# Reordering the first loads of a linear-attention and token-MLP kernel: one DMA ring held back, two weight chunks moved forward, DMA transposes held behind a copy

## The chip, the cores and the metric

The kernel runs on one core of one Trainium2 chip. The metric is the device time of one execution in microseconds (us), median over several runs. Beside it stands the profile of one execution; its span is about 1.8 us shorter than the time of the same run, and all times inside it are counted from the start of its span. The engines are PE (matrix multiply), PEld (its weight loads), DVE (vector), ACT (scalar), POOL and SP (which here only issues DMAs). DMAs are issued on two rings, SP's and ACT's. With one core there is no die to compare with, so the runs call a run slow when it is over 1.5% above the fastest of the same kernel.

## The reference, cut to what matters

```python
def reference(A_x, A_wqkv, A_wo, B_x, B_w1, B_b1, B_w2, B_b2, gate_w):
    x = A_x                                     # 1 x 2048 x 512, bf16
    g = _sigmoid((x * gate_w).sum(-1, keepdims=True))
    # a: qkv = x @ wqkv; linear attention with 32 heads and phi(t) = (t+1 if t>0 else exp(t)) + 1e-6; then @ wo
    # b: layernorm(x), then an MLP over the token axis: 2048 -> 1792 (gelu) -> 2048
    return g * a + (1 - g) * b
```

Only the beginning concerns us. It computes k = x @ Wk for one tile of 128 tokens after another, and phi(k). For this PE needs x transposed, and Wk, whose 512 rows come in four chunks of 128 (wk0 to wk3).

## The kernel before

The first four x tiles (x0 to x3) are transposed by PE, the other twelve by DMA transposes. Six dummy matmuls keep PE busy until x0 is there.

```python
    load_x(nc.sync, 0, 1)
    load_x(nc.scalar, 1, 1)
    load_wk(nc.sync, 0)
    load_x(nc.scalar, 2, 1)
    load_x(nc.sync, 3, 1)
    for k, q in ((1, nc.scalar), (2, nc.sync), (3, nc.scalar)):
        load_wk(q, k)
    load_xT(4, 2)                       # DMA transposes, all on SP's ring
    load_xT(6, 2)
    load_x(nc.sync, 4, 4)
    # ... further loads on SP's ring, cut ...
    warm_up(6)                          # dummy 128x512 matmuls

    def transpose_tile(t, on_act):      # 4 PE transposes, one copy PSUM -> SBUF
        pt = bank("pt", BF16)
        for k in range(ND):
            nc.tensor.transpose(pt[:, k * P : (k + 1) * P], xs[:, t, k * P : (k + 1) * P], ident[:])
        # ... copy by ACT if on_act, else by DVE ...

    HEADS = 4
    transpose_tile(0, False)
    transpose_tile(1, True)
    transpose_tile(2, False)
    ln_step(0)
    for k in range(2):
        for t in range(HEADS - 1):
            k_part(t, (k,))             # one matmul: tile t with wk chunk k
    transpose_tile(HEADS - 1, True)
    ln_step(1)
    for t in range(HEADS):
        k_part(t, range(2 if t < HEADS - 1 else 0, ND))
        k_phi(t)
    # for t in range(HEADS, NT): k_part(t, ...), k_phi(t), g_tile(t - LAG), ...  cut
```

Of the kernel before, what the change touches and what calls it, by code (L numbers as in the profile page):

```python
# [10 lines left out]
BF16 = mybir.dt.bfloat16  # L11
# [4 lines left out]
def kernel(  # L16
# [13 lines left out]
    nc = tc.nc  # L30
    P = nc.NUM_PARTITIONS
# [6 lines left out]
    S, D = X.shape  # L38
    F = B_w1.shape[1]
    NT = S // P  # L40
    ND = D // P
# [4 lines left out]
    FB = 4  # L46
# [4 lines left out]
    w1_chunks = [(j, min(FB, NF - j)) for j in range(0, NF, FB)]  # L51
# [3 lines left out]
    wqkv_view = A_wqkv.rearrange("(k p) n -> p k n", p=P)  # L55
    wo_view = A_wo.rearrange("(j p) n -> p j n", p=P)
    w1_view = B_w1.rearrange("(t p) f -> p t f", p=P)
# [3 lines left out]
    wpool = ctx.enter_context(tc.tile_pool(name="wstream", bufs=4))  # L61
# [5 lines left out]
    def keep(shape, dtype, name):  # L67
        return persist.tile(shape, dtype, name=name, tag=name)

    def bank(name, dtype=FP32):  # L70
        return ps.tile([P, SC], dtype, name=name, tag="bank")

    xs = keep([P, NT, D], BF16, "xs")
    hs = keep([P, NT, D], BF16, "hs")
    xT = keep([P, ND, S], BF16, "xT")
    wq_sb = keep([P, ND, D], BF16, "wq_sb")
    wk_sb = keep([P, ND, D], BF16, "wk_sb")
    wv_sb = keep([P, ND, D], BF16, "wv_sb")
    wo_sb = keep([P, ND, D], BF16, "wo_sb")
# [32 lines left out]
    def mm(o, lhsT, rhs, start, stop, **kw):  # L112
        nc.tensor.matmul(o, lhsT=lhsT, rhs=rhs, start=start, stop=stop, **kw)  # L113
# [14 lines left out]
    def load_x(q, t0, n):  # L128
        q.dma_start(out=xs[:, t0 : t0 + n, :], in_=x_view[:, t0 : t0 + n, :])

    def load_wk(q, k):
        q.dma_start(out=wk_sb[:, k, :], in_=wqkv_view[:, k, D : 2 * D])

    def load_xT(t0, n):
        nc.sync.dma_start(
            out=xT[:, :, t0 * P : (t0 + n) * P], in_=X[t0 * P : (t0 + n) * P, :], transpose=True
        )

    load_x(nc.sync, 0, 1)
    load_x(nc.scalar, 1, 1)  # L140
    load_wk(nc.sync, 0)
    load_x(nc.scalar, 2, 1)
    load_x(nc.sync, 3, 1)
    for k, q in ((1, nc.scalar), (2, nc.sync), (3, nc.scalar)):
        load_wk(q, k)
    load_xT(4, 2)
    load_xT(6, 2)
    load_x(nc.sync, 4, 4)
    for t0, n in ((8, 4), (12, 4)):
        load_xT(t0, n)  # L150
        load_x(nc.sync, t0, n)
    nc.sync.dma_start(out=wq_sb[:], in_=wqkv_view[:, :, 0:D])
    w1c = []
    for c, (j0, nb) in enumerate(w1_chunks):
        w = wpool.tile([P, NT, FB * P], BF16, name="w1c", tag="wc")
        w1c.append(w)
        for t0 in range(0, NT, 8) if c == 0 else (0,):
            t1 = t0 + 8 if c == 0 else NT
            nc.sync.dma_start(
                out=w[:, t0:t1, : nb * P], in_=w1_view[:, t0:t1, j0 * P : (j0 + nb) * P]  # L160
            )
        if c == 0:
            nc.sync.dma_start(out=wv_sb[:], in_=wqkv_view[:, :, 2 * D : 3 * D])
            nc.sync.dma_start(out=wo_sb[:], in_=wo_view)

    nc.vector.memset(ones_f[:], 1.0)
    nc.vector.memset(mhalf[:], -0.5)
    nc.vector.memset(Z32[:], 0.0)
    nc.gpsimd.memset(ident[:], 0.0)
    nc.gpsimd.affine_select(  # L170
        out=ident[:], in_=ident[:], compare_op=ALU.not_equal, fill=1.0, base=0,
# [5 lines left out]
        out=maskQ[:], in_=maskH[:].rearrange("p (a m) -> p m a", m=2), op=ALU.max, axis=AX.X  # L177
# [12 lines left out]
    def warm_up(n, cols=SC):  # L190
        for _ in range(n):
            mm(wps[:, :cols], warm[:, 0:P], warm[:, :cols], True, True)

    act_warm = keep([P, 1], FP32, "act_warm")
    nc.scalar.activation(out=act_warm[:], in_=ones_f[:], func=ACT.Exp)
    warm_up(6)

    def transpose_tile(t, on_act):
        pt = bank("pt", BF16)
        for k in range(ND):  # L200
            nc.tensor.transpose(pt[:, k * P : (k + 1) * P], xs[:, t, k * P : (k + 1) * P], ident[:])  # L201
        dst = xT[:, :, t * P : (t + 1) * P]
        src = pt[:].rearrange("p (k s) -> p k s", k=ND)
        if on_act:
            nc.scalar.activation(out=dst, in_=src, func=ACT.Copy)
        else:
            nc.vector.tensor_copy(out=dst, in_=src)
# [13 lines left out]
    def k_part(t, ks):  # L221
        if t not in kaccs:
            kaccs[t] = bank("kacc")
        for k in ks:
            mm(
                kaccs[t][:], xT[:, k, t * P : (t + 1) * P], wk_sb[:, k, :],
                k == 0, k == ND - 1,
            )

    def k_phi(t):  # L230
        phi(pk[:, t, :], kaccs.pop(t))
# [46 lines left out]
    def ln_step(u):  # L278
        ln_stats(u)
        if u % TPC == TPC - 1:  # L280
            ln_rstd(u // TPC)

    HEADS = 4
    transpose_tile(0, False)
    transpose_tile(1, True)
    transpose_tile(2, False)
    ln_step(0)
    for k in range(2):
        for t in range(HEADS - 1):
            k_part(t, (k,))  # L290
    transpose_tile(HEADS - 1, True)
    ln_step(1)
    for t in range(HEADS):
        k_part(t, range(2 if t < HEADS - 1 else 0, ND))
        k_phi(t)
    LAG = 4
    LN_LAG = 3
# [156 lines left out]
    for j in range(NB0, NF):  # L454
        c, jj = divmod(j, FB)
# [18 lines left out]
        out=gg[:], in0=gth[:], scalar1=0.5, scalar2=0.5, op0=ALU.mult, op1=ALU.add  # L474
    )
    nc.vector.tensor_scalar(
        out=c1[:], in0=gth[:], scalar1=-0.5, scalar2=0.5, op0=ALU.mult, op1=ALU.add
# [3 lines left out]
    for t in range(NT):  # L481
        c, tl = divmod(t, TPC)
        aps = bank("aps")
        for j in range(ND):
# [3 lines left out]
            out=a_sc[:], in_=aps[:], func=ACT.Identity,  # L488
            scale=gg[:, t : t + 1], bias=c2[:, t : t + 1],
        )  # L490
        for c0, W in ((0, D - P), (D - P, P)) if t == NT - 1 else ((0, D),):
            cs = slice(c0, c0 + W)
            yps = bank("yps")
            for f in range(NF):
# [6 lines left out]
                out=ot[:, :W], in0=yps[:, :W], scalar=c1[:, t : t + 1], in1=a_sc[:, cs],  # L501
# [35 lines left out]
```

## Time and profile before

| | |
|---|---|
| time, median of 3 runs (later 4) | 164.49 us (164.51), 164.18 to 164.63 |
| span of the profile | 162.6 us |
| first x tile landed, first PE transpose | 3.69 us, 3.74 us |
| PE at full clock from | 5.73 us |
| last of the eight first loads landed | 6.83 us |
| tile 4's first k matmul | 9.05 us |
| last store landed, end of the span | 161.63 us, 162.59 us |

Landings are read from the semaphore records of the trace (a semaphore is a counter on which engines wait): a load has landed when the last of its 16 increments is there. The full clock begins where the trace's clock record goes from 0.5 to 1.0.

From the page of the kernel before: PE's share (part 1), what the DMA engines moved in 40 slices of 4.07 us (part 2), and the chain that ended last, by engine and by line (part 4).

```profile
...
PE 158.0 (97%) x823; PEld 72.9 (45%) x837; DVE 89.5 (55%) x210; ACT 63.3 (39%) x97; POOL 17.5 (11%) x34
...
GB/s 141 252 247 246 278 312 355 382 386 386 281 5 0 0 0 223 228 4 0 272 324 77 209 328 323 279 106 94 32 32 32 32 32 43 48 42 33 32 32 32
...
PE 96%; DMA 2%; issue 1%; DVE 0%
PE uacc L113 30%; PE yps L113 30%; PE kacc L113 9%; PE aps L113 8%; PE gacc L113 8%; PE qacc L113 8%; DMA xs<-in_A_x_dram 2%; PE pt L201 1%; PE denps L113 1%; PE kvps L113 0%; PE w2ps L113 0%; DVE ot L500 0%; PE pt L330 0%
```

PE is busy almost all of the span. The chain's share that is not PE lies in the first microseconds. Here is that chain in order of time, for the first 10 us of the kernel before; the columns are start, duration (both us), and what.

```profile
...
0.81 2.88 DMA xs<-in_A_x_dram
3.69 0.05 issue
3.74 1.46 PE pt L201 x12
5.20 1.63 PE kacc L113 x6
6.83 0.22 PE pt L201 x4
7.05 3.02 PE kacc L113 x14
```

By this reading the kernel waits 2.88 us for x0, and then PE works without a hole.

The timeline of PE in the kernel before, 2.4 to 7.2 us: start, duration, engine, line, operation, output and inputs, count, and in brackets the idle time before it and what ended that.

```profile
...
3.74 1.46 PE L201 MATMUL pt<-ident,xs 128*128 128x128 bf16 x12 [0.17 <-DMA xs<-in_A_x_dram]
4.99 1.84 PE L113 MATMUL kacc<-wk_sb,xT 128*128 128x512 bf16 x6
6.66 0.39 PE L201 MATMUL pt<-ident,xs 128*128 128x128 bf16 x4
6.89 0.60 PE L113 MATMUL kacc<-wk_sb,xT 128*128 128x512 bf16 x2
```

Twelve transposes, six k matmuls, four transposes, then the rest. Before 5.73 us the starts of two 128x512 matmuls lie 0.427 us apart, after it 0.216 us.

The last thing to read is the end, which nobody looked at before the result. There the engines meet at two barriers: with a drain (an instruction that does no work here) an engine joins a barrier, and then it waits until the barrier is released.

### The profile page before, as it was taken

How to read it: one execution, taken by the hardware profiler on the slowest of the kernel's cores; microseconds unless marked ns; L12 is line 12 of the kernel's file. 1: busy time of each engine (PE TensorE's matmuls, PEld its weight loads, DVE VectorE, ACT ScalarE, POOL GpSimd, SP SyncE). 2: the span in 40 equal slices, each digit the busy share in tenths (PEclk: the TensorE clock that was granted, in tenths of full speed). 3: DMA queues.
4: the chain of work that ended last, by engine and by line, in shares of the span. 5: the costliest groups of instructions: out<-in, count | busy, mean ns of one | idle time of the engine just before them, and what ended most of it. 6: DMA issues, size and time to landing. Idle time of an engine off the chain costs nothing.

```text
span 162.6 us, 2183 instructions
## 1 busy us (share of the span) xinstructions
PE 158.0 (97%) x823; PEld 72.9 (45%) x837; DVE 89.5 (55%) x210; ACT 63.3 (39%) x97; POOL 17.5 (11%) x34
## 2 busy tenths in 40 slices
PE   7999999999999999999999999999999999999992
PEld 2544444444444444444444444444444444444452
DVE  0599999967999999519995401166211111111112
ACT  3463386648667483212865113111122222111110
POOL 3000711200110000001415500050000000000000
PEclk9999999999999999999999999999999999999999
DMA  4999999999900006600892699732000001110001
GB/s 141 252 247 246 278 312 355 382 386 386 281 5 0 0 0 223 228 4 0 272 324 77 209 328 323 279 106 94 32 32 32 32 32 43 48 42 33 32 32 32
DMA packets 30057, 25.05 MB, mean 154 GB/s; under 512 B 7968, under 2 KB 29472, under 8 KB 30048
## 3 DMA queue, kind: packets, MB, share of 16 engines
q1 hardware_dynamic: 28032, 22.02, 42.9%
q0 software_dynamic: 1440, 2.38, 5.5%
q10 hardware_dynamic: 576, 0.52, 1.1%
q8 instruction: 6, 0.10, 0.2%
q14 instruction: 3, 0.02, 0.1%
HBM read 21.11 MB, written 2.23 MB: 144 GB/s over the span
## 4 chain that ended last, share of the span: by engine, by line
PE 96%; DMA 2%; issue 1%; DVE 0%
PE uacc L113 30%; PE yps L113 30%; PE kacc L113 9%; PE aps L113 8%; PE gacc L113 8%; PE qacc L113 8%; DMA xs<-in_A_x_dram 2%; PE pt L201 1%; PE denps L113 1%; PE kvps L113 0%; PE w2ps L113 0%; DVE ot L500 0%; PE pt L330 0%
## 5 line engine op out<-in xcount | busy, mean ns | idle before, releaser
L113 PE MATMUL uacc<-hs,w1c 128*128 128x512 bf16 x219 | 51.0, 379 | 0.4
L113 PE MATMUL yps<-uT,w2c 128*128 128x512 bf16 (+2 forms) x234 | 50.6, 366 | 0.2
L500 DVE SCALAR_TENSOR_TENSOR ot<-yps,c,a_sc 128x512 bf16<-128x512 f32 (+2 forms) x17 | 12.2, 719 | 44.8 <-PE yps L113 41.5
L113 PEld LDWEIGHTS <-w2c 128*128 128x128 bf16 x238 | 22.8, 98 | 25.9
L113 PEld LDWEIGHTS <-w1c 128*128 128x128 bf16 x224 | 21.8, 98 | 26.3 <-issue 0.2
L487 ACT ACTIVATE a_sc<-aps,c,gg 128x512 f32<-128x512 f32 x16 | 12.4, 777 | 46.7 <-PE aps L113 43.0
L324 ACT ACTIVATE uT<-uacc,bcol 128x512 bf16<-128x512 f32 x14 | 9.3, 688 | 21.7 <-PE uacc L113 21.7
L113 PE MATMUL aps<-W2sb,pqT 128*128 128x512 bf16 x63 | 16.2, 379 | 0.1
L113 PE MATMUL qacc<-xT,wq_sb 128*128 128x512 bf16 x63 | 16.2, 379 | 0.0
L113 PE MATMUL kacc<-wk_sb,xT 128*128 128x512 bf16 x63 | 16.1, 385 | 0.0
L113 PE MATMUL gacc<-pk,xs 128*128 128x512 bf16 x62 | 15.5, 379 | 0.1
L251 ACT ACTIVATE hs<-xs,nmr,rstd 128x512 bf16<-128x512 bf16 x16 | 12.8, 805 | 1.9 <-DVE nmr L245 1.9
L211 ACT ACTIVATE e<-qacc 128x512 bf16<-128x512 f32 x16 | 9.6, 597 | 9.2 <-PE qacc L113 8.3
L211 ACT ACTIVATE e<-kacc 128x512 bf16<-128x512 f32 x16 | 9.3, 595 | 6.9 <-PE kacc L113 5.6
L439 POOL DMA_DIRECT2D rex<-rd_dram x16 | 9.4, 598 | 22.9 <-DVE pqT L441 20.1
L215 DVE SCALAR_TENSOR_TENSOR pqT<-qacc,e 128x512 bf16<-128x512 f32 x16 | 11.1, 692 | 0.6
L215 DVE SCALAR_TENSOR_TENSOR pk<-kacc,e 128x512 bf16<-128x512 f32 x16 | 11.1, 692 | 0.6
L235 DVE BATCH_NORM_STATS2 stats<-xs 128x6 f32<-128x512 bf16 x16 | 10.9, 682 | 0.0
L212 DVE TENSOR_SCALAR e<-e 128x512 bf16<-128x512 bf16 x32 | 9.0, 282 | 3.2 <-ACT e L211 3.2
L426 DVE CUSTOM_DVE_ANT_0 junk<-xs,gw_b 128x512 bf16<-128x512 bf16 x16 | 9.8, 684 | 0.0
L276 DVE TENSOR_TENSOR zacc<-zacc,pk 128x512 f32<-128x512 f32 x14 | 9.6, 685 | 0.2
L113 PEld LDWEIGHTS <-pqT 128*128 128x128 bf16 x64 | 6.3, 98 | 7.6
(61 smaller groups left out, 71.7 us busy)
## 6 DMA issues: line engine op xcount, KB each, us to landing
w2c<-in_B_w_dram SPq DMA_DIRECT2D x8, 896.0 KB, 6.1
w1c<-in_B_w_dram SPq DMA_DIRECT2D x2, 2048.0 KB, 14.7
w1c<-in_B_w_dram SPq DMA_DIRECT2D x3, 1024.0 KB, 11.9
rex<-rd_dram POOLq DMA_DIRECT2D x16, 128.0 KB, 4.0
out_dram<-ot SPq DMA_DIRECT2D x15, 128.0 KB, 1.7
xs<-in_A_x_dram SPq DMA_DIRECT2D x3, 512.0 KB, 4.4
wq_sb<-in_A_wqkv_dram SPq DMA_DIRECT2D x1, 512.0 KB, 6.3
wv_sb<-in_A_wqkv_dram SPq DMA_DIRECT2D x1, 512.0 KB, 11.8
```

The source lines that it names most:

```text
L113: nc.tensor.matmul(o, lhsT=lhsT, rhs=rhs, start=start, stop=stop, **kw)
L211: nc.scalar.activation(out=e[:], in_=acc[:], func=ACT.Exp)
L212: nc.vector.tensor_scalar(out=e[:], in0=e[:], scalar1=1.0, scalar2=PHI_EPS, op0=ALU.min, op1=ALU.add)
L215: nc.vector.scalar_tensor_tensor(out=dst, in0=acc[:], scalar=0.0, in1=e[:], op0=ALU.max, op1=ALU.add)
L235: nc.vector.bn_stats(out=stats[:], in_=xs[:, t, :])
L251: nc.scalar.activation(out=hs[:, t, :], in_=xs[:, t, :], func=ACT.Identity, scale=rstd[:, t : t + 1], bias=nmr[:, t : t + 1],)
L276: nc.vector.tensor_tensor(out=zacc[:], in0=first, in1=pk[:, t, :], op=ALU.add)
L324: nc.scalar.activation(out=uT[:, j, :], in_=acc[:], func=ACT.Gelu_apprx_tanh, bias=bcol[:, j : j + 1])
L426: nc.vector.tensor_tensor_reduce(out=junk[:], in0=xs[:, t, :], in1=gw_b[:], scale=1.0, scalar=0.0, op0=ALU.mult, op1=ALU.add, accum_out=gp ...
L439: nc.gpsimd.dma_start(out=rex[:], in_=src.unsqueeze(1).to_broadcast([8, HEAD, SC]))
L487: nc.scalar.activation(out=a_sc[:], in_=aps[:], func=ACT.Identity, scale=gg[:, t : t + 1], bias=c2[:, t : t + 1],)
L500: nc.vector.scalar_tensor_tensor(out=ot[:, :W], in0=yps[:, :W], scalar=c1[:, t : t + 1], in1=a_sc[:, cs], op0=ALU.mult, op1=ALU.add,)
```

## The change

Its intent: let x0, which PE needs first, have the DMA engines to itself (ACT's first load waits for a tiny memset); bring wk0 and wk1 right after x0 and x1 and contract them for two tiles before x2 and x3 are transposed; and keep the DMA transposes out of the way until the first copy is done. The core of the diff, with cuts:

```diff
+    def hold(dst):
+        nc.vector.memset(dst, 0.0)
+    nc.vector.memset(ones_f[:], 1.0)
+    nc.vector.memset(mhalf[:], -0.5)
+    nc.vector.memset(Z32[:], 0.0)
+    hold(xs[:, 1, 0:2])                      # x1's load (ACT's ring) waits for this
     load_x(nc.sync, 0, 1)
     load_x(nc.scalar, 1, 1)
     load_wk(nc.sync, 0)
-    load_x(nc.scalar, 2, 1)
-    load_x(nc.sync, 3, 1)
-    for k, q in ((1, nc.scalar), (2, nc.sync), (3, nc.scalar)):
-        load_wk(q, k)
+    load_wk(nc.scalar, 1)
+    load_x(nc.sync, 2, 1)
+    load_x(nc.scalar, 3, 1)
+    load_wk(nc.sync, 2)
+    load_wk(nc.scalar, 3)
 ... (definitions moved up, unchanged but for transpose_part, which copies chunks k0 to k1 of a tile)
-    warm_up(6)
+    warm_up(5)
+    transpose_part(0, 0, 1, False)
+    hold(xT[:, :, 4 * P : 4 * P + 2])        # the DMA transposes wait for this
     load_xT(4, 2)
     load_xT(6, 2)
 ...
-    transpose_tile(0, False)
-    transpose_tile(1, True)
-    transpose_tile(2, False)
+    transpose_part(0, 1, ND, False)
+    transpose_part(1, 0, 1, False)
+    transpose_part(1, 1, ND, False)
+    for k in range(2):
+        for t in range(2):
+            k_part(t, (k,))
     ln_step(0)
-    for k in range(2):
-        for t in range(HEADS - 1):
-            k_part(t, (k,))
-    transpose_tile(HEADS - 1, True)
+    transpose_part(2, 0, ND, False)
+    transpose_part(3, 0, ND, True)
     ln_step(1)
     for t in range(HEADS):
-        k_part(t, range(2 if t < HEADS - 1 else 0, ND))
+        k_part(t, range(2 if t < 2 else 0, ND))
         k_phi(t)
```

More of the change, by code (lines that the diff above doesn't have):

```diff
@@ L141 @@
     load_wk(nc.sync, 0)
-    load_x(nc.scalar, 2, 1)
-    load_x(nc.sync, 3, 1)
-    for k, q in ((1, nc.scalar), (2, nc.sync), (3, nc.scalar)):
-        load_wk(q, k)
-    load_xT(4, 2)
-    load_xT(6, 2)
-    load_x(nc.sync, 4, 4)
-    for t0, n in ((8, 4), (12, 4)):
-        load_xT(t0, n)
-        load_x(nc.sync, t0, n)
-    nc.sync.dma_start(out=wq_sb[:], in_=wqkv_view[:, :, 0:D])
-    w1c = []
-    for c, (j0, nb) in enumerate(w1_chunks):
-        w = wpool.tile([P, NT, FB * P], BF16, name="w1c", tag="wc")
-        w1c.append(w)
-        for t0 in range(0, NT, 8) if c == 0 else (0,):
-            t1 = t0 + 8 if c == 0 else NT
-            nc.sync.dma_start(
-                out=w[:, t0:t1, : nb * P], in_=w1_view[:, t0:t1, j0 * P : (j0 + nb) * P]
-            )
-        if c == 0:
-            nc.sync.dma_start(out=wv_sb[:], in_=wqkv_view[:, :, 2 * D : 3 * D])
-            nc.sync.dma_start(out=wo_sb[:], in_=wo_view)
-    nc.vector.memset(ones_f[:], 1.0)
-    nc.vector.memset(mhalf[:], -0.5)
-    nc.vector.memset(Z32[:], 0.0)
+    load_wk(nc.scalar, 1)
[3 more added lines that the diff above has]
+    load_wk(nc.scalar, 3)
     nc.gpsimd.memset(ident[:], 0.0)
@@ L195, with transpose_part @@
     nc.scalar.activation(out=act_warm[:], in_=ones_f[:], func=ACT.Exp)
-    warm_up(6)
-    def transpose_tile(t, on_act):
+    warm_up(5)
+    def transpose_part(t, k0, k1, on_act):
         pt = bank("pt", BF16)
-        for k in range(ND):
+        for k in range(k0, k1):
             nc.tensor.transpose(pt[:, k * P : (k + 1) * P], xs[:, t, k * P : (k + 1) * P], ident[:])
-        dst = xT[:, :, t * P : (t + 1) * P]
-        src = pt[:].rearrange("p (k s) -> p k s", k=ND)
+        dst = xT[:, k0:k1, t * P : (t + 1) * P]
+        src = pt[:, k0 * P : k1 * P].rearrange("p (k s) -> p k s", k=k1 - k0)
         if on_act:
@@ L283 @@
     HEADS = 4
-    transpose_tile(0, False)
-    transpose_tile(1, True)
-    transpose_tile(2, False)
+    transpose_part(0, 0, 1, False)
+    hold(xT[:, :, 4 * P : 4 * P + 2])
+    load_xT(4, 2)
+    load_xT(6, 2)
+    load_x(nc.sync, 4, 4)
+    for t0, n in ((8, 4), (12, 4)):
+        load_xT(t0, n)
+        load_x(nc.sync, t0, n)
+    nc.sync.dma_start(out=wq_sb[:], in_=wqkv_view[:, :, 0:D])
+    w1c = []
+    for c, (j0, nb) in enumerate(w1_chunks):
+        w = wpool.tile([P, NT, FB * P], BF16, name="w1c", tag="wc")
+        w1c.append(w)
+        for t0 in range(0, NT, 8) if c == 0 else (0,):
+            t1 = t0 + 8 if c == 0 else NT
+            nc.sync.dma_start(
+                out=w[:, t0:t1, : nb * P], in_=w1_view[:, t0:t1, j0 * P : (j0 + nb) * P]
+            )
+        if c == 0:
+            nc.sync.dma_start(out=wv_sb[:], in_=wqkv_view[:, :, 2 * D : 3 * D])
+            nc.sync.dma_start(out=wo_sb[:], in_=wo_view)
+    transpose_part(0, 1, ND, False)
[4 more added lines that the diff above has]
+            k_part(t, (k,))
     ln_step(0)
-    for k in range(2):
-        for t in range(HEADS - 1):
-            k_part(t, (k,))
-    transpose_tile(HEADS - 1, True)
+    transpose_part(2, 0, ND, False)
+    transpose_part(3, 0, ND, True)
     ln_step(1)
     for t in range(HEADS):
-        k_part(t, range(2 if t < HEADS - 1 else 0, ND))
+        k_part(t, range(2 if t < 2 else 0, ND))
         k_phi(t)
```

## The prediction

> **What bounds the kernel.** PE: busy 97% of the 162.6 us span (page, part 1) and 96% of the chain that ended last (part 4). From about 5.8 us the timeline shows matmuls back to back, one 128x512 every 0.216 us, to the end. DVE (55%), ACT (39%) and DMA have slack after the start. Only the start can give anything: the 2.88 us in which the chain waits for the first x tile, the half-clock stretch, and a few waits on copies.
>
> **The start before (timeline and landings in the trace).** Both rings issue at 0.80 us. ACT's packets flow first (1.83 us), SP's from 2.19; x1 (ACT) lands at 3.50, x0 (SP) at 3.69, though PE needs x0 first. Six warm-up matmuls end about 3.56; transposes start at 3.74. x2 and wk0 land at 4.13 and 4.32, but wk1, x3, wk3, wk2 only at 5.85, 6.06, 6.57, 6.83: the DMA transposes, issued at 3.52, get in between. PE runs at half speed until 5.73 (transposes 0.107 us apart, 128x512 0.427), then at full speed (0.055 and 0.216). PE waits in this stretch are under 0.3 us together. Tile 4's first kacc matmul starts at 9.05 us.
>
> **What the change does.**
> - ACT's first issue waits for a small memset: about 1.15 instead of 0.80 us. x0 flows alone first. Estimate, shifting its packets by the 0.36 us that separate the rings: x0 at 3.3 us (-0.4), x1 at 3.6. The Trainium skill, "DMA: Bandwidth & Descriptors", Issuing engines are not separate DMA queues, says that both rings share the 16 engines; the interleaved packets here agree.
> - wk0 and wk1 move second: about 4.0 and 4.3 us.
> - The DMA transposes wait for the first copy (about 3.9 us), so the last loads finish about 0.5 us sooner and tile 4's xT 0.4 later, 8.1 us, still before its use.
> - One warm-up fewer: PE idles from about 3.1 to 3.3.
> - Tile 1's copy moves from ACT (0.60 us) to DVE, and tiles 0 and 1 are copied in two parts: about +0.55 us DVE, before its first phi, where it waited 0.93 us.
> - Order: 8 transposes, 4 kacc, 8 transposes, then dense, against 12, 6, 4.
>
> **How much is on the critical path.** PE's work from first transpose to tile 4 is unchanged: 16 x 0.055 + 16 x 0.216 = 4.3 us at full speed. Starting 0.4 us earlier, while the clock is at half, is worth only 0.2 us. Some 0.05 to 0.1 us of that can go to waits on the smaller copies and wk0; the removed waits of before give as much. I expect tile 4's first matmul at about 8.85 us (-0.2), everything after it shifted by the same, nothing lost later.
>
> **Prediction.** 164.3 us (before 164.49), range 163.75 to 164.85; faster by over 2%: 0.005, within 2%: 0.985, slower by over 2%: 0.01.
>
> **What would show it.** x0 landing near 3.3 and before x1; first transpose near 3.35; wk1, wk2, wk3 before 6.4; full clock from about 5.7; tile 4's first kacc near 8.85; then the same 0.216 us rhythm.
>
> **What would make it wrong.** The full clock may come at another time: the skill's "TensorE: Matmul & The Clock Gate", Part 1, says it follows sustained activity in a free-running window (the one switch here, at 5.73 us, cannot show this). An idle gap before x0, or another phase of the window, would move the end by half of the shift: more than the change itself. Or x0 does not land sooner when alone; or the held DMA transposes reach tile 4 late.

## More of the kernel before

The drains and waits of SP's closing block in the kernel before, from 161.70 to 162.3 us: line, engine, operation, count, shortest/median/longest in ns, first and last start.

```profile
L532 SPq DRAIN  x2: 7/10/13, 161.7 to 161.8; - x2
L532 SPq EVENT_SEMAPHORE  x1: 17/17/17, 162.3 to 162.3; - x1
```

## The result, and the profile after

The changed kernel took 164.64 us (median of 4 runs: 164.63, 164.64, 164.65 and one of 167.18 us that counts as slow), the kernel before 164.51 us. The ratio is 1.0011, with a 95% interval of 0.9991 to 1.0031. Ratios are computed from the mean time of one kernel's fast runs over that of the other's in the same rounds, so they are not quite the ratio of the medians quoted. No change beyond noise. The span of the profile is 162.9 us, 0.3 more.

First the start. The chain in order of time, first 10 us of the changed kernel:

```profile
...
1.12 0.41 ACTq L129
1.53 0.03 issue
1.56 3.58 DMA wk_sb<-in_A_wqkv_dram
5.14 0.04 issue
5.18 0.59 PE kacc L113 x2
5.78 0.51 PE pt L186 x8
6.29 3.61 PE kacc L113 x16
...
```

The chain no longer goes through x0, but through a chunk of Wk that was issued at 1.56 us and landed at 5.14. PE's timeline, 2.4 to 7.2 us of the changed kernel, shows why:

```profile
...
2.98 1.20 PE L186 MATMUL pt<-ident,xs 128*128 128x128 bf16 x8
3.98 1.80 PE L113 MATMUL kacc<-wk_sb,xT 128*128 128x512 bf16 x4
5.61 0.68 PE L186 MATMUL pt<-ident,xs 128*128 128x128 bf16 x8
6.13 1.40 PE L113 MATMUL kacc<-wk_sb,xT 128*128 128x512 bf16 x5
```

Transposes start at 2.98 us instead of 3.74, and eight of them, four k matmuls and eight more are done by 6.13. But four 128x512 matmuls do not fill 1.8 us, nor five 1.4 us: PE waited about 0.35 us for wk1 (landed 5.14) and 0.16 us for wk3 (landed 6.46). A group's duration in this view covers its holes.

Tile 4's first k matmul starts at 8.87 us, 0.18 us earlier than before. And from there to the last store nothing is lost. The timeline of DVE after 158 us, kernel before and changed kernel; it makes the last two output pieces:

```profile
...
159.05 1.08 DVE L500 SCALAR_TENSOR_TENSOR ot<-yps,c,a_sc 128x384 bf16<-128x384 f32 x2 [2.39 <-PE yps L113]
```

```profile
...
158.87 1.08 DVE L508 SCALAR_TENSOR_TENSOR ot<-yps,c,a_sc 128x384 bf16<-128x384 f32 x2 [2.39 <-PE yps L113]
```

The last store lands at 161.45 instead of 161.63 us, still 0.18 us earlier. Yet the span ends 0.31 us later, so about 0.49 us went in the last 1.5 us, after all work was done. SP's closing block in the changed kernel, from 161.52 to 162.3 us:

```profile
L540 SPq DRAIN  x2: 13/72/130, 161.5 to 162.0; - x2
L540 SPq EVENT_SEMAPHORE  x1: 17/17/17, 162.3 to 162.3; - x1
```

The two drains, 0.06 us apart before, are now 0.46 us apart, and one takes 130 ns. Here are SP's last instruction records, counted from SP's first record, with start times in us:

```
record  kernel before                          changed kernel
78      161.724 drain                          161.469 wait for the last stores
79      161.784 drain (SP joins barrier 1)     161.549 drain
80      162.254 wait (barrier 1 released)      162.010 drain (SP joins barrier 1)
81      162.359 drain (SP joins barrier 2)     162.285 wait (barrier 1 released)
82      162.528 wait (barrier 2 released)      162.377 drain (SP joins barrier 2)
83                                             162.835 wait (barrier 2 released)
```

In both kernels record 80 comes about 0.45 us after the end of record 79. In the kernel before, that is the wait behind barrier 1: the other engines pass the barrier at 161.94, POOL then works on its own until 162.27, and the pause is nearly hidden behind that. In the changed kernel SP has one instruction more, and record 80 is the drain with which SP joins barrier 1: everyone waits for it. The additional instruction is at 2.950 us in the trace: the first DMA transpose now has two semaphores to wait for, and one of the two waits is an instruction of its own.

That gives two theories to test. **Tail:** a pause of about 0.45 us belongs to SP's 80th recorded instruction; the change moved it to where it is paid. Its rival: the late end is chance, or comes of the clock or the stores. **Start:** the start is bound by the landing of the last of the eight loads (in the kernel before, wk2 landed at 6.83 us, just when PE came to use it). Its rival is the prediction's: PE's own work from x0 on, part of it at half clock, decides.

### The profile page after: what moved, and what is told of

Read it like the earlier page. It is cut to its first block, busy times and chain, and to the rows that moved or that the text cites. A ratio compares the mean times of both kernels' runs of the same rounds, so it can differ in the third digit from the quotient of the medians.

```text
span 162.9 us, 2188 instructions
## 1 busy us (share of the span) xinstructions
PE 157.8 (97%) x822; PEld 72.5 (44%) x836; DVE 90.2 (55%) x215; ACT 63.0 (39%) x96; POOL 17.5 (11%) x34
## 4 chain that ended last, share of the span: by engine, by line
PE 94%; DMA 2%; issue 1%; DVE 0%; ACTq 0%
PE yps L113 30%; PE uacc L113 29%; PE qacc L113 9%; PE aps L113 8%; PE gacc L113 8%; PE kacc L113 8%; DMA wk_sb<-in_A_wqkv_dram 2%; PE denps L113 1%; PE kvps L113 0%; PE pt L186 0%; ACTq L129 0%; PE w2ps L113 0%; DVE ot L508 0%; DVE Z L144 0%; DVE ones_f L142 0%
## 5 line engine op out<-in xcount | busy, mean ns | idle before, releaser
L113 PE MATMUL kacc<-wk_sb,xT 128*128 128x512 bf16 x64 | 16.7, 387 | 0.1
L113 PEld LDWEIGHTS <-xT 128*128 128x128 bf16 x64 | 6.3, 99 | 7.9 <-DVE stats L220 0.6
```

Source lines behind the costliest of these rows:

```text
L113: nc.tensor.matmul(o, lhsT=lhsT, rhs=rhs, start=start, stop=stop, **kw)
```

## The experiments

Twelve runs, each five rounds, beside the kernel before on the same chip. The four kernels of the first call, and the fill, warm-up and five-load kernels of the third, ran on one chip, the others on a second one. A drain on SP, put where SP has nothing to do (about 33 to 60 us), serves as a neutral additional instruction. By the 2% rule the verdict of every run is the same, no change; what is read below are smaller differences, from the intervals and the traces. One caution: runs of 166 to 167 us count as slow only where they are over 1.5% above the fastest of their kernel. Four of the ratios below hold such runs (the changed kernel again, wk3 last, two warm-ups, 40 drains); with all runs above 166 us left out, the plain means give 1.003, 1.002, 1.004 and 1.000.

```diff
+    for _ in range(6):
+        nc.sync.drain()
+
     NB0 = 3
```

### The tail

**The changed kernel again.** No edit.

> The changed kernel unaltered, a second sample. Theory (one more SP instruction moves a pause of about 0.4 us at the 80th recorded SP instruction from behind the closing barrier to in front of it): the same pause at the same instruction, last output landed about 0.18 us earlier than in the kernel before, span still about 162.9, time about 164.6. Rival (the late end was chance in one trace): SP's first closing drain follows within 0.1 us of the one ahead of it, span about 162.4, time about 164.2. Full clock: if its moment is tied to the kernel's start, 5.0 us again; if it is of a free phase, another value.

Measured: 165.0 us median (164.91 to 165.26, and one of 167.09), kernel before 164.59; ratio 1.0053 (1.001 to 1.0096). The pause is again at record 80, 0.45 us; the span is longer than expected (163.5), since the loads landed later: wk3 only at 7.09 us. The chain of this run, first 12 us, its largest DMA piece and what follows:

```profile
...
2.20 4.67 DMA wk_sb<-in_A_wqkv_dram
6.92 3.61 PE kacc L113 x16
...
```

Full clock came at 4.59 us, not at 5.0: its moment is not tied to the kernel's start.

**The changed kernel with 6 drains.** The edit above.

> The changed kernel with 6 drains added on SP while SP has nothing to do (about 33 to 60 us). Theory (pause at the 80th recorded SP instruction): the pause now falls among the waits for the last outputs, which SP spends waiting anyway, and costs nothing: span about 162.4, time about 164.15, 0.4 to 0.5 under the changed kernel. Rival (the tail is chance, or comes of the clock, or of the last store): as the changed kernel, 164.6.

Measured: 164.38 us (164.16 to 164.64), 0.62 us under the changed kernel of the same rounds; ratio to the kernel before 0.9993 (0.9974 to 1.0012). The pause (0.46 us) is at record 80 again, which is now one of the waits for the last stores. From the last landing to the end 0.91 us instead of 1.45. SP's closing block in this run, 160.8 to 162.2 us:

```profile
L543 SPq EVENT_SEMAPHORE  x9: 28/28/28, 160.9 to 161.9; - x9
L543 SPq DRAIN  x2: 7/7/7, 162.0 to 162.1; - x2
```

The two drains are 0.06 us apart. The tail theory holds. The span missed its number (162.8, not 162.4), because this run's last wk chunk landed at 6.93 us and its last store at 161.93.

**The kernel before with 1 drain.** The same edit with `range(1)`, in the kernel before.

> The kernel before with 1 drain added on SP while it is idle. Theory (pause at the 80th recorded SP instruction): the pause moves in front of the closing barrier and is paid in full: about 164.9, 0.3 to 0.4 over the kernel before, with the start and all of PE unchanged. Rival: 164.5, unchanged.

Measured: 165.15 us (164.68 to 165.22), ratio 1.0032 (1.0012 to 1.0052). From the last landing to the end 1.44 us instead of 0.96. SP's closing block, 162.05 to 162.9 us:

```profile
L535 SPq DRAIN  x2: 7/69/131, 162.1 to 162.5; - x2
L535 SPq EVENT_SEMAPHORE  x1: 17/17/17, 162.8 to 162.8; - x1
```

One idle instruction, with the start left as it was, makes the same tail as the changed kernel's. The rival of the tail theory falls.

**The kernel before with 7 drains.** The same edit with `range(7)`, in the kernel before.

> The kernel before with 7 drains added on SP while it is idle, so that it has as many SP instructions as the changed kernel with 6. Theory: the pause is hidden among the waits for the last outputs: 164.4 to 164.5, 0 to 0.1 under the kernel before; against the changed kernel with 6 drains it shows what the start alone is worth, 0.15 to 0.25 us. Rival: 164.5, and no difference of the two beyond noise but 0.1 the other way, as between the two kernels without drains.

Measured: 164.33 us (164.18 to 164.61), ratio 0.9991 (0.9972 to 1.001). Against the changed kernel with 6 drains, with the same number of SP instructions and the pause hidden in both, the means are 164.37 and 164.41 us. The expected 0.15 to 0.25 us in favour of the new start is a miss: with the tail out of the way, the new start is worth nothing that 6 runs can see.

### The start

All that follows are edits of the changed kernel with 6 drains, with the pause hidden (SP's instruction count was kept by adding drains where an edit took one away).

**ACT's ring not held.**

```diff
-    hold(xs[:, 1, 0:2])
```

> The changed kernel with 6 idle drains (164.38 us), less the memset that holds ACT's ring. New theory (the start is bound by the landing of the last of the eight loads, not by the first x tile): x1 lands at about 3.5 and x0 at 3.7 as before, the first transpose slips from 2.98 to 3.74, but the last wk chunk still lands at 6.5 to 7.0 and tile 4 starts 2.4 us after it: time unchanged, within 0.15 us. Rival (as predicted blind: start of PE and half clock decide): 0.2 to 0.4 us slower.

Measured: 164.35 us (163.91 to 164.78), kernel before 164.44, ratio 0.9999 (0.9979 to 1.0019). x1 lands at 3.56 and x0 at 3.75, transposes start at 3.80, 0.8 us later than with the hold. The last wk chunk lands at 6.92. The chain of this run, first 12 us:

```profile
...
2.22 4.70 DMA wk_sb<-in_A_wqkv_dram
6.97 3.61 PE kacc L113 x16
...
```

The 0.8 us of earlier transposes that the hold buys are worth nothing: the new theory's number, and not the rival's 0.2 to 0.4 us slower.

**DMA transposes not held.**

```diff
-    hold(xT[:, :, 4 * P : 4 * P + 2])
```

> The changed kernel with idle drains on SP, less the memset that holds the DMA transposes (7 drains, so as many SP instructions as with 6). The transposes issue at about 2.95 instead of 3.58 us. Theory 1 (the transposes' descriptors and packets slow the loads that are still under way): wk1 to wk3 land 0.2 to 0.6 us later, tile 4 and the end by as much later: 164.6 to 164.9. Theory 2 (the loads are slow for another reason): landings of wk1 at 5.1 to 5.5 and of wk3 at 6.5 to 7.1 as ever, time unchanged within 0.15 us of 164.38.

Measured: 165.89 us (164.08 to 166.77; the profiled run counts as slow), ratio 1.0072 (1.0035 to 1.0109). In its profile SP issued the first transpose at 2.67 us, and ACT issued its fourth load (wk3) at 3.05 us instead of 2.53; wk3 landed at 8.49. The edit did more than it says: in this program wk3's load uses the semaphore of x0's load, and its issue waits for that one (x0 landed at 3.03); in the changed kernel it waits for nothing. Its chain, first 12 us, shows the wait:

```profile
...
3.05 5.44 DMA wk_sb<-in_A_wqkv_dram
8.49 0.04 issue
8.54 3.60 PE kacc L113 x13
```

So this variant is slower, but the earlier transposes and the later issue of wk3 came together, the only profile of it is of a slow run, and its full clock came at 9.85 us besides: how much each of the three costs is not told, nor whether the hold alone is needed. The five unheld runs that are slow or nearly so stand against one of 164.08 us.

**DMA transposes held longer**, behind the fourth copy. The three other copies are moved ahead of the hold:

```diff
     transpose_part(0, 0, 1, False)
+    transpose_part(0, 1, ND, False)
+    transpose_part(1, 0, 1, False)
+    transpose_part(1, 1, ND, False)
     hold(xT[:, :, 4 * P : 4 * P + 2])
```

> The changed kernel with 6 idle drains, the DMA transposes held behind the fourth copy (about 4.6 us) instead of the first (3.58). Theory 1 (transposes slow the loads): wk1 lands before 4.8, the last wk chunk before 6.0, tile 4's xT at about 8.6; tile 4 starts at 8.6 or before: 0.2 to 0.5 us faster than 164.38. Theory 2 (another reason): wk1 at 5.1 to 5.5 and the last wk chunk at 6.4 to 7.0 as ever, and no gain.

Measured: 164.35 us (163.68 to 164.76, and one slow run of 166.2), ratio 0.9991 (0.9967 to 1.0016). The transposes were issued at 4.58 us; wk1 landed at 5.52 and the last chunk at 6.76, as late as ever. Theory 2 holds in this profile: beyond the hold of the change, the transposes are not what makes the loads late.

**wk3's four matmuls last.**

```diff
     for t in range(HEADS):
-        k_part(t, range(2 if t < 2 else 0, ND))
+        k_part(t, range(2 if t < 2 else 0, ND - 1))
+    for t in range(HEADS):
+        k_part(t, (ND - 1,))
         k_phi(t)
```

> The changed kernel with 6 idle drains; the four matmuls with wk chunk 3 are put after all others of tiles 0 to 3, so that only 4 matmuls (0.86 us) instead of 11 (2.4 us) wait for the last load. Theory (bound by the last load): tile 4 starts about 8.3 to 8.7 us instead of 8.9 to 9.3: 0.2 to 0.5 us faster than 164.38. Rival (PE's own work bounds): unchanged within 0.1 us, or slower, if the later phi of tiles 0 and 1 holds up DVE.

Measured: 164.87 us (164.43 to 165.06, and one of 166.74), ratio 1.0045 (1.0008 to 1.0083): not faster, a miss. Tile 4's first k matmul did not start early either, at 9.04 us, though the last load was there at 6.42. No load held it in this profile: PE has no hole from 4.11 us on, and its full clock came only at 6.17 us, so here the rival is right, PE's own work at half clock decides. And then PE met a new wait. The waits of this run between 9 and 14 us: engine, line, what it waited for, us in total, times, longest.

```profile
...
PEld L113 <- DVE pk L200: 0.7, 1, 0.7
PE gacc L113 <- DVE pk L200: 0.2, 1, 0.2
...
```

phi of tile 0 comes later in this order, and the next product needs it: its first matmul starts 1.26 us after tile 4's first, where the changed kernel has 0.86. So more than one limit stands close behind the loads.

**Two warm-up matmuls instead of five.**

```diff
-    warm_up(5)
+    warm_up(2)
```

> The changed kernel with 6 idle drains and 2 warm-up matmuls instead of 5, so that PE idles from about 1.7 to 3.0 us, before x0 lands. Theory (idle PE early on puts off the full clock, which is what the rare runs of 166 to 167 us are): the profile shows the full clock later than 6.3 us, the latest of any fast profile so far, and the runs are slower on the whole, median over 164.9, several at 165.5 to 167. Rival (the start is bound by the loads and the rare slow runs come of DMA): median 164.3 to 164.5, full clock at 4.0 to 6.3 us as ever.

Measured: 164.98 us (164.46 to 165.48, and one of 166.64), kernel before 164.31, ratio 1.0052 (1.0016 to 1.0088). Full clock came at 6.64 us in the profile, later than in any other profile of a fast run (4.05 to 6.25). Idle PE before x0 seems to cost: about 1.0 us of ratio between this and the changed kernel with 6 drains (0.0059 of 164.5), in different rounds, or 0.7 us without the run of 166.64 (0.0044). By the rival it should have cost nothing. How it costs is not shown: the profiled run is the fastest of the six, 164.46 us, with tile 4 at 9.25.

**Two fillers while PE waits for wk1.**

```diff
             k_part(t, (k,))
+        if k == 0:
+            warm_up(2)
```

> The changed kernel with 6 idle drains and 2 more warm-up matmuls between the contractions with wk0 and wk1, where PE waits 0.35 to 0.8 us for wk1. Theory (idle PE there can put off the full clock): no run over 165.5, median unchanged at 164.2 to 164.5, since the fillers end before or just after wk1 lands. Rival (the idle there does not matter): rare slow runs as before, about one in seven, median unchanged or up to 0.2 slower.

Measured: 164.55 us (163.92 to 164.87), ratio 1.0009 (0.9988 to 1.003), no run over 165. Six runs do not tell "none" from "one in seven"; inconclusive.

**Five loads instead of eight** for the same 1 MB (wk as two loads of 256 KB, x2 and x3 in one).

```diff
-    load_wk(nc.sync, 0)
-    load_wk(nc.scalar, 1)
-    load_x(nc.sync, 2, 1)
-    load_x(nc.scalar, 3, 1)
-    load_wk(nc.sync, 2)
-    load_wk(nc.scalar, 3)
+    load_wk(nc.sync, 0, 2)          # two chunks
+    load_x(nc.scalar, 2, 2)
+    load_wk(nc.sync, 2, 2)
```

> The changed kernel with idle drains (8, so as many SP instructions as with 6), wk in two loads of 256 KB and x2 with x3 in one, 5 loads instead of 8 for the same 1 MB. Theory 1 (the number of small loads and their issue slows them; what takes 4.6 us for 1 MB is not bandwidth[...]): the last of them lands before 5.9 us instead of 6.4 to 7.1, tile 4 starts 0.3 to 0.6 us earlier, 163.9 to 164.2. Theory 2 (bytes or a slow stretch of memory at 4 to 5 us): the last lands at 6.4 to 7.1 as ever, time unchanged, or slower by up to 0.4, since wk0 now waits for wk1.

Measured: 164.70 us (164.15 to 164.87), ratio 1.0017 (0.9999 to 1.0035). The last load landed at 6.60 us, in the range of all others. It is not the number of loads. (Its tail is 1.11 us, as here the last store landed soon after the pause and three waits still followed.)

**wk3 of tiles 0 to 2 behind their others, and 40 drains.**

```diff
-    for t in range(HEADS):
-        k_part(t, range(2 if t < 2 else 0, ND))
+    for t in range(HEADS - 1):
+        k_part(t, range(2 if t < 2 else 0, ND - 1))
+    for t in range(HEADS):
+        k_part(t, range(ND - 1 if t < HEADS - 1 else 0, ND))
         k_phi(t)
```

> The changed kernel with 40 idle drains on SP, and the matmuls with wk chunk 3 of tiles 0 to 2 put after their others (tile 3 last), so that 7 matmuls instead of 11 wait for the last load. Two readings, apart in the trace. Tail: if the pause belongs to the 80th recorded SP instruction, it now falls near 106 us, between two stores, and from the last landing to the end there are about 0.85 to 0.95 us (1.45 in the changed kernel); if it belongs to the end of the program, it stays at the end. Start: if the last load bounds it, tile 4 starts 0.2 to 0.5 us earlier than 8.9 to 9.3 and the time is 164.0 to 164.3; if DVE's phi of tiles 0 and 1 takes over, as where all four went last, nothing is gained: 164.4 or more.

Measured: 164.55 us (164.04 to 164.55 and two of 166.3 and 166.47), ratio 1.0055 (1.0009 to 1.0101). The tail reading is clear: record 80 is now at 106.78 us, between two stores, with a pause of 0.45 us before it; the closing block has none, and the end comes 0.90 us after the last landing. SP's closing block of this run, 161.40 to 161.8 us:

```profile
L545 SPq DRAIN  x3: 7/7/7, 161.5 to 161.8; - x3
...
```

The pause goes with the instruction's number, not with the end of the program. What else goes with it stands in the DMA records. The DMA view of the changed kernel from 162.4 to 162.9 us and of this run from 106.9 to 108 us (queue and kind: packets, MB, share of 16 engines):

```profile
q14 instruction: 1, 0.01, 6.9%
...
q14 instruction: 1, 0.01, 2.7%
```

In each of the 14 traces one packet of 8,192 bytes of the kind "instruction" starts 0.56 to 0.93 us after the start of record 80: at 162.66 us in the changed kernel, at 163.18 in the kernel before (after the end of its span), at 107.43 here. It moves with the drains as the pause does, so the pause very likely belongs to a fetch of SP's instructions. That the fetch causes it is not shown: the packet starts when record 80 has already run, and the trace does not name the engine that it is for.

The start gained little in the profile (tile 4 at 8.81 us, last load at 6.37) and nothing in the median. No version tried beats the kernel before beyond noise; the kernel before with 7 drains and the changed kernel with 6 drains and later transposes come nearest (0.9991 both), and both intervals include 1.

### What the profiles say together

Last of the first loads landed, and tile 4's first k matmul, in us. The third column counts the k matmuls from the one that needs that chunk to the last before tile 4:

| profile | last load | matmuls from it on | tile 4 | difference |
|---|---|---|---|---|
| before | 6.83 | 10 | 9.05 | 2.22 |
| before, 7 drains | 6.57 | 9 | 8.96 | 2.39 |
| changed | 6.46 | 11 | 8.87 | 2.41 |
| changed, again | 7.09 | 11 | 9.50 | 2.41 |
| changed, 6 drains | 6.93 | 11 | 9.35 | 2.41 |
| ditto, transposes late | 6.76 | 11 | 9.18 | 2.41 |
| ditto, ACT not held | 6.92 | 12 | 9.55 | 2.63 |

The difference is the number of matmuls times 0.216 us plus 0.03 to 0.06 us, in all but the second row. In these six the first transpose, from 2.98 to 3.80 us, and the full clock, from 4.05 to 6.25, do not enter (in the kernel before, PE's own work came out at the same moment). In the second row another load decides: PE's last hole ended with wk1 (landed 5.89), and 13 k matmuls and 4 transposes behind it, about 3.0 us, lead to 8.96; wk3 landed 0.45 us before it was used.

The other seven profiles do not follow the rule of the last load either, but for the one with unheld transposes. With 1 drain in the kernel before, and with 40 drains, PE's last hole before tile 4 ended with wk1 (6.35 and 5.27), and with five loads it ended with x2 and x3 (6.34). With wk3 last, with two warm-ups and with fillers, the profiles with the full clock at 6.17, 6.64 and 6.04 us, the last two loads held nothing, and PE's own work, part of it at half clock, decided. So neither theory of the start holds alone: tile 4 comes when both the loads and PE's work are through, and the two lie within a few tenths of a microsecond. In the changed kernel as measured it was the last load.

The last load, with x0 early or not, lands somewhere between 6.4 and 7.1 us from run to run (8.49 in the one with unheld transposes). That scatter of 0.7 us is larger than anything the change did to the start.

From its first packet at 1.83 us to 6.83, that 1 MB moves at 210 GB/s (1,048,576 bytes in 5.0 us), against 386 GB/s in the best slices of the same profile. Order, ring hold, number of loads, and a longer hold of the transposes left it there. What does hold it back stays open.

Also open are the rare runs above 166 us. Among the 52 runs of kernels with x0 early (without the one with unheld transposes) there are 7; among the 56 of the kernel before, its two drain variants and the variant without ACT's hold there are none. That idle PE in the first microseconds puts off the full clock would explain them, and the medians of the warm-up experiment speak for it, but no trace of such a run with held transposes was taken.

## Why the prediction was right or wrong

The time was right: 164.3 us with a range of 163.75 to 164.85, measured 164.64, and "within 2%" was nearly certain. But a gain of 0.19 us was forecast and a loss of 0.13 us measured, inside a range of 1.1 us: that the number came out right says little for the sum behind it. Point by point:

- *PE bounds the kernel; only the start can give anything.* The first half stands. The second fell: the end could take. The step that failed is "everything after it shifted by the same, nothing lost later". PE and the last store were shifted by 0.18 us, but the end lost 0.49 us to SP's pause. That term was missing from the sum, and it is the larger one. A count of SP's instructions, 82 against 83, and a look at the last microsecond of the trace of before, where SP's 80th record comes 0.46 us after the 79th, would at least have raised the question.
- *x0 at 3.3 us.* Mis-sized: 2.93 us, and 2.83 to 3.03 in all runs with ACT held. The direction and the mechanism (alone on the engines, it lands sooner) were right.
- *wk1 about 4.3 us, the last loads 0.5 us sooner because the DMA transposes are held.* Failed: wk1 landed at 5.14, and at 4.83 to 5.56 in the other profiles with both holds and eight loads. The blame laid on the transposes' issue is not borne out: a second microsecond of hold changed nothing. Only the variant that issued them at 2.67 us, earlier than the kernel before (3.52 to 3.75), was slower, and there wk3's issue was put off too.
- *Tile 4 at 8.85 us.* Measured 8.87, right by accident. The prediction got 0.2 us from starting 0.4 us earlier at half clock. The trace got it from a last load 0.37 us earlier with one matmul more behind it (0.22 us). The repeat, with its last load at 7.09, has tile 4 at 9.50: no gain but a loss of 0.46 us.
- *Full clock from about 5.7 us, perhaps elsewhere.* 5.0, 4.59 and 4.05 us in the three profiles with the same start. The warning was right; but where loads bound the start, an earlier clock gives nothing.
- *Tile 4's DMA transposes in time.* Right: landed at 7.53, first used at 8.87 us.

## What to carry to other kernels

When an engine is made to start earlier, ask for the last thing that the stage needs and how much work stands behind it, not for the first: here a first tile 0.76 us earlier bought nothing that the times show, since in the changed kernel the last of eight loads came when it came. A chain of waits names one path; a second one of equal length, as wk2 beside PE here, does not show until the first is shortened. And when a change is worth a few tenths of a microsecond, compare the traces to the very last record, and count the instructions of the idle engines too: one wait more on SP cost more than the whole start could give.

## What the Trainium skill lacked or had wrong

- No page gives the size of a pause like the one found here: SP's 80th recorded instruction started 0.44 to 0.53 us after the end of the 79th in all 14 profiles, wherever in time it lay (106.8 to 163.8 us), and paid in full before the closing barrier it costs about 0.5 us. "Runtime: NRT & Kernel Launch", section Instruction fetch mechanics, says that an engine's instructions are fetched in blocks of 256 and that crossing a block is mostly hidden. The traces fit such a crossing, one instruction packet of 8,192 bytes 0.56 to 0.93 us after record 80 in all 14, but there it was hidden only where SP had time to spare. Why it is the 80th recorded instruction stays open.
- "DMA: Bandwidth & Descriptors", section Issuing engines are not separate DMA queues, agrees with the runs (both rings' packets interleave, and the order of the rings only chose who came first: x0 at 2.93 us with ACT held, 3.35 to 3.75 in the profiles without). It lacks what the first loads of a program get: 1 MB landed at 6.4 to 7.1 us in eight loads or in five.
- "TensorE: Matmul & The Clock Gate", Part 1, is borne out in its rates and its window: matmuls 0.427 and 0.216 us apart, full clock at 4.05 to 6.64 us in the profiles of fast runs, and the stretches at full clock last 157.01 or 160.43 us, which are 46 and 47 times the page's window of 3413 ns. For modelling it puts the ramp's penalty under 1% of a typical kernel's span. The runs agree, but that can still be more than the whole change at issue: with two warm-up matmuls instead of five, the ratio to the kernel before was 1.0052 instead of 0.9993.
